# A searched order of 950 steps replaced by another one: the same instructions on all engines, with the groups of many small products kept apart

## The chip, the cores and the metric

The kernel runs on one core of a Trainium2 chip. A core has five engines with a queue of instructions each: PE (TensorE, matmuls and their weight loads), DVE (VectorE), ACT (ScalarE), POOL (GpSimd) and SP (SyncE, which here only issues DMAs). Each engine takes its own queue strictly in order; where an instruction needs what another engine or a DMA makes, it waits for a semaphore, and all that is behind it in its queue waits too. The metric is the device time of one execution in microseconds (us), as a median of several executions. The span of a profile is a little shorter than the time of the execution that it shows.

## The reference

The result is a sum of three terms over a sequence of 2048 tokens with 512 channels: the input itself, a state-space convolution of its layernorm, and a gated linear unit of its layernorm.

```python
x  = A_u                                    # [1, 2048, 512], bf16
xn = _layernorm(x)

# A: diagonal state space, 128 modes a channel, as a convolution of length 2048
dt = exp(log_dt)[:, None]
K  = einsum("dn,dnl,dn->dl", Cc, exp(dt * A * l), dt * Bc).real
y  = irfft(rfft(pad(xn)) * rfft(pad(K)))[:L] + xn * Dskip

# B: gated linear unit, 512 -> 1792 -> 512
g, u = xn @ w_gate, xn @ w_up
b    = (sigmoid(g) * u) @ w_down

return x + y + b
```

## The kernel before

**What is computed how.** The gated unit works on four groups of 512 tokens. For each group there are 14 blocks of 128 hidden units. A block takes four matmuls for the gate (line 1013, 128x512, accumulated over 4 pieces of the 512 channels) and four for the up-projection (L1037). ACT makes the sigmoid of the gate (L1025), DVE multiplies it with the up-projection (L1052). For some blocks ACT first copies the up-projection out of the matmul's memory (L1048), and the product on DVE is then cheaper. The blocks for which that is so are listed in `UEV`. When the 14 products of a group are there, 4 times 14 matmuls (L1086) with `wd_sb`, the weights w_down, make the output.

The convolution is computed by a transform written as small matmuls. The layernormed input goes through a first stage (L683, groups of eight 32-row matmuls), is copied by ACT (L285) and stored to scratch memory in HBM (`z_scr`). From there it is loaded again in 16 units of 256 channels by 8 frequency groups, transformed (L875, four matmuls), multiplied with the transformed kernel (L897 makes the kernel's part from the loaded table `c_E`; DVE multiplies on L902 and L906), transformed back (L919, 16 matmuls) and stored (`v_scr`), to be read at the end by the last stage (L979).

The kernel K of the convolution is made from powers of the 128 modes. This is done four times, for 128 channels each. DVE builds two tables of powers by complex products (L722, L723, L727, L728, with squares from ACT L775). PE then multiplies them in two halves of 64 small products each (L806, 32 columns, 82 moving elements, each with a weight load of its own); ACT or DVE copies both halves out (L285 or L283, 128x656), and PE selects and sorts the entries by 64 more small products (L826). Their result is copied out (128x768), and DVE adds one row to it (L837). L806 and L826 are the groups of many small products. All of these tables, and the transforms' steps, share the two wide buffers `pair0` and `pair1` of the matmul memory.

The layernorm of each 128 tokens ends in a scaling, on DVE (L555) or on ACT (L550), as the list `ON_DVE` says. Tokens from 512 on are transposed by way of HBM: SP stores 512 scaled tokens to `x_scr` (L418), and a transposing load brings them back as `xnT` (L573), which the gate's and up-projection's matmuls of the groups 1 to 3 read.

**What sets the order.** The program builds a list of 950 steps (`pl.add`, `pl.copy`, `dma`), each with its engine and a function that issues its instructions. `ORDER` is a list of the 950 numbers, written out. `_Plan.run` goes through it: it gives each step its buffers from the pools in that order, and the steps' functions are then called one after the other. So `ORDER` fixes the order of instructions in each engine's queue, the order of the DMAs that SP issues, and which buffer of a pool each step has. Nothing reorders it afterwards.

```python
for n in ORDER or range(len(self.ops)):
    op = self.ops[n]
    for s in op.acq:
        s.idx = self.free[s.pool].pop(0)
    for s in op.rel:
        self.free[s.pool].append(s.idx)
    yield op
```

`ON_DVE` lists the steps among the copies and the late layernorm scalings that go to DVE and not to ACT. Of the numbers that it holds, 103 to 132 are scalings, 360 a copy of 128x656, 362 one of 128x768, 516 and 520 ones of 128x1024, and 843 to 853 ones of 128x512.

The DMAs on SP are issued in `ORDER`'s order as well (L418 for all of them, L573 for the transposing loads). `wd_sb` is loaded by one DMA of 1.8 MB.

Of the kernel before, what the change touches and what calls it, by code (L numbers as in the profile page):

```python
# [180 lines left out]
def _consts():  # L181
# [19 lines left out]
UEV = (0, 2, 4, 5, 6, 7, 9, 10, 11, 12, 13, 14, 15, 16, 17, 20, 21, 23, 24, 25, 26, 27, 28, 29, 30, 31, 32, 33, 34, 35, 36, 37, 38, 39, 40, 41, 42, 43, 44, 47, 49, 50, 55,)  # L201
ON_DVE = (103, 105, 116, 132, 360, 362, 516, 843, 853,)
ON_ACT = (2,)
ORDER = [
# [50 lines left out]
class _Plan:  # L255
# [20 lines left out]
    def copy(self, nc, cost, out, in_, *args, **kw):  # L276

        get = lambda v: v() if callable(v) else v
        dve = len(self.ops) in ON_DVE

# [35 lines left out]
def kernel(  # L316
# [214 lines left out]
    def layernorm(i0, i1, prio):  # L531
# [14 lines left out]
        for i in range(i0, i1):  # L546
            dve = i < LN_ACT or len(pl.ops) in ON_DVE
            if not dve:
# [448 lines left out]
    for grp in range(4):  # L997
        hts, prods = [], []
        for u2 in range(7):
# [4 lines left out]
            for k in (2 * u2, 2 * u2 + 1):  # L1004
# [38 lines left out]
                us = _Slot("us")  # L1043
                on = un in UEV

# [136 lines left out]
```

## Time and profile before

| What | Value |
|---|---|
| median of 3 runs | 219.53 us (218.43 to 220.34) |
| the profiled execution's own time | 219.73 us |
| its span | 217.9 us |
| busy PE | 209.3 us (96% of the span), 2098 matmuls |
| busy DVE | 199.7 us (92%), 439 instructions |
| busy ACT | 171.4 us (79%), 277 instructions |
| busy POOL | 33.4 us (15%) |
| bytes moved by DMA | 44.46 MB, 204 GB/s in the mean |

An engine is busy while one of its instructions runs; the rest of the span it waits, or has nothing left. A matmul counts from its start to an end that is modelled, and matmuls overlap, so that the distance from one start to the next says more than the duration of one. In a list of pieces in order of time, a row holds the start, the length, the engine, the line, what it writes and reads, and how many instructions are merged in it; a bracket at its end says how long the engine was idle before it and who ended that. "issue" there means that the profile shows nothing for which the engine waited.

### The profile page before, as it was taken

The numbers are of one execution on the slowest core, as the hardware profiler recorded it, in microseconds if no ns is written. First come the engines' busy times: TensorE is split into PE (matmuls) and PEld (weight loads), VectorE is DVE, ScalarE is ACT, GpSimd is POOL, SyncE is SP. The second block draws the span as 40 slices with busy tenths as digits, with TensorE's granted clock in tenths as the row PEclk, the third lists the DMA queues.
The fourth block names the chain that finished last, engine by engine and source line by source line (L and its number), as shares of the span: only waits on it lengthen the run. The fifth ranks groups of instructions, "written<-read, shape, count | busy, mean of one in ns | idle before, by whom it ended". The sixth has DMA issues, their size and how long they took to land.

```text
span 217.9 us, 5440 instructions
## 1 busy us (share of the span) xinstructions
PE 209.3 (96%) x2098; PEld 104.2 (48%) x2098; DVE 199.7 (92%) x439; ACT 171.4 (79%) x277; POOL 33.4 (15%) x65
## 2 busy tenths in 40 slices
PE   7999999999999999997999999899989999999995
PEld 2654443444444544443655555454546465544453
DVE  4999999999999999999799999999989999984673
ACT  3799999999999997797899999667659979752000
POOL 3125153145104000108100000000010100000200
PEclk9999999999999999999999999999999999999999
DMA  5999999629988678479546343970996876888744
GB/s 173 339 427 433 280 203 161 94 67 191 275 208 182 195 252 237 123 188 288 102 129 205 96 147 87 254 215 3 271 276 144 305 188 200 224 238 222 218 173 144
DMA packets 44044, 44.46 MB, mean 204 GB/s; under 512 B 9449, under 2 KB 35314, under 8 KB 43890
## 3 DMA queue, kind: packets, MB, share of 16 engines
q1 hardware_dynamic: 39330, 39.06, 57.9%
q0 software_dynamic: 4384, 4.73, 13.7%
q10 hardware_dynamic: 304, 0.33, 0.6%
q8 instruction: 16, 0.26, 0.5%
q14 instruction: 10, 0.08, 0.1%
HBM read 25.22 MB, written 12.07 MB: 171 GB/s over the span
## 4 chain that ended last, share of the span: by engine, by line
PE 54%; ACT 23%; DMA 11%; issue 5%; SPq 3%; DVE 2%; POOL 0%; ACTq 0%; POOLq 0%
PE bank L1086 15%; PE bank L1013 10%; PE bank L1037 8%; ACT big L285 8%; PE pair L897 7%; ACT hT_sb L1025 5%; PE pair L919 4%; PE bank L521 3%; ACT us_sb L1048 3%; SPq L418 3%; DMA xnT<-x_scr 2%; DMA x_scr<-big 2%; DMA z_scr<-big 2%; DMA big<-z_scr 2%; ACT big L655 2%
## 5 line engine op out<-in xcount | busy, mean ns | idle before, releaser
L285 ACT ACTIVATE big<-pair 128x1024 bf16<-128x1024 f32 (+2 forms) x73 | 71.1, 1005 | 10.2 <-PE pair L919 3.4
L1037 PE MATMUL bank<-xnT,wu_sb 128*128 128x512 bf16 x224 | 53.9, 380 | 0.0
L1013 PE MATMUL bank<-xnT,wg_sb 128*128 128x512 bf16 (+1 forms) x220 | 51.6, 368 | 0.9 <-DMA xnT<-x_scr 0.5
L1086 PE MATMUL bank<-wd_sb,hT_sb 128*128 128x512 bf16 (+1 forms) x238 | 50.9, 367 | 0.0
L1086 PEld LDWEIGHTS <-hT_sb 128*128 128x128 bf16 x238 | 22.7, 98 | 24.9 <-issue 1.8
L1025 ACT ACTIVATE hT_sb<-bank 128x512 bf16<-128x512 f32 x52 | 31.0, 613 | 4.6 <-PE bank L1013 4.3
L1013 PEld LDWEIGHTS <-wg_sb 128*128 128x128 bf16 x236 | 21.7, 98 | 25.2 <-issue 3.0
L1037 PEld LDWEIGHTS <-wu_sb 128*128 128x128 bf16 x224 | 20.7, 98 | 25.3 <-issue 2.5
L1048 ACT ACTIVATE us_sb<-bank 128x512 bf16<-128x512 f32 x43 | 26.3, 617 | 2.4 <-PE bank L1037 2.4
L722 DVE TENSOR_TENSOR big<-big 128x1024 bf16<-128x1024 bf16 (+4 forms) x40 | 26.5, 663 | 0.7 <-ACT big L285 0.6
L723 DVE TENSOR_TENSOR big<-big 128x1024 bf16<-128x1024 bf16 (+4 forms) x40 | 26.4, 660 | 0.0
L897 PE MATMUL pair<-big 128*128 128x256 bf16 x160 | 19.6, 273 | 0.9 <-DMA big<-c_E 0.9
L902 DVE TENSOR_TENSOR big<-big 128x2048 bf16<-128x2048 bf16 x16 | 19.5, 1220 | 0.4
L897 PEld LDWEIGHTS <-big 128*128 128x128 bf16 x160 | 15.4, 98 | 6.0 <-DMA big<-c_E 1.4
L1052 DVE TENSOR_TENSOR hT_sb<-hT_sb,us_sb 128x512 bf16<-128x512 bf16 x43 | 17.4, 414 | 0.7 <-ACT us_sb L1048 0.7
L660 POOL DMA_DIRECT2D big<-big x24 | 13.1, 551 | 25.4 <-DVE big L666 23.4
L775 ACT ACTIVATE sq_sb<-big 128x256 bf16<-128x256 bf16 (+2 forms) x20 | 13.4, 676 | 3.9 <-DVE big L728 3.9
L727 DVE TENSOR_TENSOR big<-big 128x512 bf16<-128x512 bf16 (+4 forms) x40 | 16.3, 407 | 0.2
L728 DVE TENSOR_TENSOR big<-big 128x512 bf16<-128x512 bf16 (+4 forms) x40 | 16.3, 408 | 0.0
L285 ACT ACTIVATE big<-big 128x256 bf16<-128x256 bf16 x36 | 15.6, 474 | 0.0
L888 DVE COPY big<-big 32x1024 bf16<-32x1024 bf16 x32 | 13.4, 420 | 0.5
L919 PE MATMUL pair<-big 64*64 64x512 bf16 (+1 forms) x256 | 13.0, 326 | 0.2 <-ACT big L285 0.2
(100 smaller groups left out, 214.2 us busy)
## 6 DMA issues: line engine op xcount, KB each, us to landing
big<-c_E SPq DMA_DIRECT2D x16, 320.0 KB, 3.9
z_scr<-big SPq DMA_DIRECT2D x16, 256.0 KB, 3.9
big<-z_scr SPq DMA_DIRECT2D x16, 256.0 KB, 4.2
v_scr<-big SPq DMA_DIRECT2D x16, 256.0 KB, 2.5
big<-big POOLq DMA_DIRECT2D x24, 128.0 KB, 3.6
big<-in_A_u_dram SPq DMA_DIRECT2D x4, 512.0 KB, 6.8
big<-big SPq DMA_DIRECT2D x32, 64.0 KB, 3.3
big<-v_scr SPq DMA_DIRECT2D x4, 512.0 KB, 4.7
```

The source lines that it names most:

```text
L285: nc.scalar.activation(out=get(out), in_=get(in_), func=ACT.Identity)
L722: V.tensor_tensor(out=wide(outp), in0=wide(lo), in1=mre, op=ALU.mult)
L723: V.tensor_tensor(out=wide(tb()), in0=wide(lo), in1=mim, op=ALU.mult)
L897: T.matmul(two(sk)[:, o:o + DW], es()[:, g, kt, :], kT[p][:, kt, :], start=kt in (0, NKT - 1), stop=kt >= NKT - 2)
L902: V.tensor_tensor(out=pp().rearrange("p q h m -> p (q h) m"), in0=xx().rearrange("p q h m -> p (q h) m"), in1=kb()[:, 0:2 * DW].unsqueeze( ...
L919: T.matmul(two(sv)[o:o + 64, DW * (2 * g + y):2 * DW * (g + 1)], mab[b:b + 64, 2 * u + g, q, :], pq()[b:b + 64, q, ch] if y else pp()[b:b ...
L1013: T.matmul(bank(sl, k % 2)[:, c0:c1], w_at(w, CUT_G, kt, k), xnT[:, grp, kt, c0:c1], start=(kt == 0), stop=(kt == KT - 1))
L1025: S.activation(out=hT_sb[:, hs.idx, k % 2, :], in_=bank(sl), func=ACT.Sigmoid)
L1037: T.matmul(bank(sl), w_at(wu_sb, CUT_U, kt, k), xnT[:, grp, kt, :], start=(kt == 0), stop=(kt == KT - 1))
L1048: S.activation(out=us_sb[:, us.idx, :], in_=bank(sl), func=ACT.Identity)
L1052: V.tensor_tensor(out=h(), in0=h(), in1=us_sb[:, us.idx, :] if on else bank(sl), op=ALU.mult)
L1086: T.matmul(bank(po)[:, 0:c[1] - c[0]], hT_sb[:, hts[k // 2].idx, k % 2, jj * 128:(jj + 1) * 128], wd_sb[:, k, c[0]:c[1]], start=first and ...
```

## The change

`ORDER` is another order of the same 950 steps. `UEV` and `ON_DVE` change with it. Everything else in the file is the same. Both kernels issue the same transfers and the same matmuls.

```diff
-UEV = (0, 2, 4, 5, 6, 7, 9, 10, 11, 12, 13, 14, 15, 16, 17, 20, 21, 23, 24, 25, 26, 27, 28, 29, 30, 31, 32, 33, 34, 35, 36, 37, 38, 39, 40, 41, 42, 43, 44, 47, 49, 50, 55,)
-ON_DVE = (103, 105, 116, 132, 360, 362, 516, 843, 853,)
+UEV = (0, 1, 2, 3, 4, 5, 6, 7, 9, 10, 11, 14, 15, 16, 17, 18, 19, 20, 21, 22, 23, 26, 27, 28, 29, 30, 31, 32, 33, 34, 35, 36, 37, 38, 39, 40, 41, 42, 44, 45, 50, 51, 52, 54, 55,)
+ON_DVE = (104, 105, 106, 119, 129, 362, 520, 843, 851,)
 ORDER = [
-    1, 0, 19, 2, 4, 3, 31, 6, 10, 32, 23, 34, 7, 33, 39, 24, 5, 25, 35, 26, 36, 11, 40, 37, 13, 20, 27, 41, 9, 51, 28, 12,
...
-    902, 931, 597, 847, 855, 930, 848, 934, 929, 856, 849, 857, 591, 932, 935, 933, 683, 675, 936, 938, 684, 937, 676,
...
+    0, 1, 20, 2, 3, 4, 23, 6, 19, 10, 24, 31, 26, 7, 25, 39, 32, 5, 33, 27, 34, 40, 11, 28, 13, 51, 35, 41, 9, 29, 36, 30,
...
+    592, 597, 847, 855, 848, 934, 856, 849, 929, 930, 857, 591, 683, 675, 684, 935, 932, 938, 676, 685, 933, 677, 936, 937,
...
```

What moves with it, as far as the prediction speaks of it:

- Between the two halves of L806 and the L826 that follows, PE has other groups in its queue. Their matmuls, for the four times: 56, 12, 32 and 24 in the old order, 56, 20, 38 and 36 in the new one. In the second time these are four of L1013, four of L1037 and four of L875 in the old order, and five groups of four of L1013 or L1037 in the new one. In the fourth they are 16 of L919, four of L875 and four of L1013 in the old order; the new one adds two large groups and one of L875.
- On SP, `wd_sb` (step 16) stands before the first store to `x_scr` (step 107) in the old order, and behind that store and the first transposing load (step 108) in the new one. The last 512 tokens of the input (step 15) are loaded before that store and not behind it.
- On DVE, the products of the first token group stand in another order among the products and scalings that build the power tables. Ahead of the fourth L806, DVE has the same steps in both orders, except for one scaling more and one product that goes from the dearer to the cheaper kind.
- `UEV` has 45 blocks where it had 43. `ON_DVE` has five late scalings (it had four), one copy of 128x768, one of 128x1024 and two of 128x512 (as before), and no longer the one of 128x656.

75 rows, old and new, of the table ORDER are left out of this document.

## The prediction

> **What bounds the kernel now.** I read the page first, then the busy time by stretches, then the idle pieces of TensorE (PE), the stretches around its groups of small products, and the waits of VectorE (DVE).
>
> ```profile
> span 217.9 us, 5440 instructions
> PE 209.3 (96%) x2098; PEld 104.2 (48%) x2098; DVE 199.7 (92%) x439; ACT 171.4 (79%) x277; POOL 33.4 (15%) x65
> ...
> 60.00:80.00 20.00, 20.00 (x239) 8.96 (x238) 20.00 (x53) 20.00 (x36) 2.63 (x8) 1.00 0.81 214
> ...
> 100.00:120.00 20.00, 18.46 (x185) 10.19 (x183) 18.59 (x39) 17.71 (x33) 4.05 (x7) 1.00 0.61 166
> 120.00:140.00 20.00, 19.39 (x325) 10.11 (x323) 19.93 (x52) 18.76 (x33) 0.35 (x2) 1.00 0.47 131
> 140.00:160.00 20.00, 18.53 (x320) 10.11 (x321) 18.98 (x36) 12.86 (x18) 0.00 (x0) 1.00 0.67 194
> ```
>
> The columns of a stretch are its length, then busy PE, weight loads, DVE, ACT, POOL, clock, DMA. Two engines are full at once: PE 209.3 of 217.9 us, and DVE 20.00 of 20 us at 60 to 80, 19.93 at 120 to 140. The granted clock is 1.00 throughout. So the time is PE's 209.3 plus what PE stands idle, and DVE is close behind. PE's idle pieces, in brackets with the releaser:
>
> ```profile
> 1.43 4.84 PE L521 MATMUL bank<-glu_sb 128*128 128x512 bf16 x14 [1.43 <-POOL glu_sb L514]
> 16.91 1.89 PE L1013 MATMUL bank<-xnT,wg_sb 128*128 128x512 bf16 x8 [0.17 <-ACT hT_sb L1025]
> 35.28 1.04 PE L1013 MATMUL bank<-xnT,wg_sb 128*128 128x512 bf16 x4 [0.49 <-DMA xnT<-x_scr]
> 102.89 0.47 PE L826 MATMUL pair<-big,sw 128*32 128x96 bf16 x26 [1.53 <-issue]
> 140.25 1.26 PE L897 MATMUL pair<-big 128*128 128x256 bf16 x10 [0.86 <-DMA big<-c_E]
> 155.19 0.84 PE L919 MATMUL pair<-big 64*64 64x512 bf16 x16 [0.21 <-ACT big L285]
> 159.10 0.31 PE L826 MATMUL pair<-big,sw 128*32 128x96 bf16 x12 [1.02 <-issue]
> ```
>
> They add up to 5.7 us; the rest of 217.9 - 209.3 = 8.6 is, but for tenths, the end, after PE's last matmul. The two largest behind the start fall inside a selection group (L826, 64 matmuls), with no releaser. Beside them stand the kernel-table products (L806, 128 matmuls with a weight load each) that precede each selection:
>
> ```profile
> 73.94 1.50 PE L806 MATMUL pair<-big 128*32 128x82 bf16 x128
> ...
> 85.03 0.86 PE L826 MATMUL pair<-big,sw 128*32 128x96 bf16 x64
> ...
> 97.23 1.42 PE L806 MATMUL pair<-big 128*32 128x82 bf16 x128
> 98.58 1.04 PE L1013 MATMUL bank<-xnT,wg_sb 128*128 128x512 bf16 x4
> 99.45 1.03 PE L1037 MATMUL bank<-xnT,wu_sb 128*128 128x512 bf16 x4
> 100.41 0.41 PE L875 MATMUL pair<-big,m 64*64 64x512 bf16 x4
> 100.75 0.60 PE L826 MATMUL pair<-big,sw 128*32 128x96 bf16 x38
> ...
> 126.17 1.59 PE L806 MATMUL pair<-big 128*32 128x82 bf16 x128
> ...
> 131.48 0.86 PE L826 MATMUL pair<-big,sw 128*32 128x96 bf16 x64
> ...
> 153.57 1.41 PE L806 MATMUL pair<-big 128*32 128x82 bf16 x128
> ...
> 157.35 0.74 PE L826 MATMUL pair<-big,sw 128*32 128x96 bf16 x52
> ```
>
> From the start of L806 to the start of its L826 there are 11.09, 3.52, 5.31 and 3.78 us. The second and fourth stalled, after 38 and 52 of 64 matmuls; the others ran through in 0.86. So it is the crowding that stalls, and the point lies between 3.78 and 5.31 us.
>
> What runs out is, I argue, instructions.
>
> ```profile
> q8 instruction: 16, 0.26, 0.5%
> ```
>
> 16 packets carry 0.26 MB; PE has 2 x 2098 instructions, so one packet is about 262 of them, which L806 alone (256) uses up in 1.4 us.
>
> The Trainium skill (Runtime: NRT & Kernel Launch, section Instruction fetch mechanics) gives the block as 16 KiB or 256 instructions, which this row bears out. The same section says that fetching is hidden, because dispatch is slower than the fill, and gives PE a store of 2048 instructions; by that the 1.53 and 1.02 would have another cause and the order would leave them, the third rival below. The rows speak against it: both stalls come only in the crowded groups.
>
> **The change, part by part.**
>
> *Spacing.* In the new order five groups of four 128x512 matmuls stand between the second L806/L826 pair where L1013, L1037 and L875 stood. A large group takes 99.45 - 98.58 = 0.87, L875 0.34 (100.41 to 100.75), so the distance becomes 3.52 - 0.34 + 3 x 0.87 = 5.8. The fourth gains two large groups and one L875: 3.78 + 2 x 0.87 + 0.34 = 5.9. The third goes from 32 matmuls between to 38, the first stays. All are beyond the 5.31 that ran through. Removed: 1.53 + 1.02 = **2.55** of PE. If a stall were only shortened, the loss is bounded by these.
>
> *What is late next: DVE.* The fourth L806 waits for DVE, as its first weight load shows; and DVE was itself idle in front of the two rows below it, and of the last one after it:
>
> ```profile
> 153.57 1.27 PEld L806 LDWEIGHTS <-big 128*32 128x32 bf16 x128 [0.42 <-DVE hT_sb L1052]
> ...
> 104.25 0.28 DVE L837 TENSOR_TENSOR big<-pair,dskr 1x128 bf16<-1x128 f32 x1 [0.78 <-ACT big L285]
> ...
> 107.03 0.39 DVE L722 TENSOR_TENSOR big<-big 128x256 bf16<-128x256 bf16 x1 [0.56 <-ACT big L285]
> ...
> 159.53 0.96 DVE L283 CAST big<-pair 128x768 bf16<-128x768 f32 x1 [0.69 <-PE pair L826]
> ```
>
> L837 comes after ACT's copy of what the stalled L826 makes, so 0.78 of DVE's idle time is the stall passed on; the 0.56 that follows within 3 us, also behind ACT, may be. DVE's work ahead of 153.57 changes too. The page's groups give the prices:
>
> ```profile
> L1052 DVE TENSOR_TENSOR hT_sb<-hT_sb,us_sb 128x512 bf16<-128x512 bf16 x43 | 17.4, 414 | 0.7 <-ACT us_sb L1048 0.7
> L1048 ACT ACTIVATE us_sb<-bank 128x512 bf16<-128x512 f32 x43 | 26.3, 617 | 2.4 <-PE bank L1037 2.4
> L1052 DVE TENSOR_TENSOR hT_sb<-hT_sb,bank 128x512 bf16<-128x512 bf16 x13 | 8.6, 679 | 1.0 <-PE bank L1037 1.0
> L550 ACT ACTIVATE big<-big,ln_nb_f,ln_ri_f 128x512 bf16<-128x512 bf16 x8 | 6.5, 831 | 0.0
> L555 DVE TENSOR_SCALAR big<-big,ln_m_f,ln_ri_f 128x512 bf16<-128x512 bf16 x8 | 3.1, 404 | 0.1
> L285 ACT ACTIVATE big<-pair 128x656 bf16<-128x656 f32 x7 | 5.1, 750 | 1.9 <-PE pair L806 1.9
> L283 DVE CAST big<-pair 128x656 bf16<-128x656 f32 x1 | 0.8, 842 | 0.2 <-ACT big L285 0.2
> ```
>
> Five late layernorm scalings instead of four go to DVE: +0.40 there, -0.83 on ACT. Two more products read a copy made by ACT: 2 x (0.414 - 0.679) = -0.53 on DVE, 2 x 0.617 = +1.23 on ACT. One 128x656 copy goes over to ACT: -0.84 and +0.75. The other copies change places one for one. Sum: DVE -0.97, ACT +1.15; ACT has 46 us free. Ahead of the fourth L806 stand 37 cheap products and 5 dear ones instead of 36 and 6, and the extra scaling: 0.40 - 0.27 = +0.14. So DVE is there 0.78 - 0.14 = 0.64 earlier, or 1.20 with the 0.56. PE has the same matmuls ahead of it in both orders, and keeps only that much of its 1.53; I take **1.0**, nearer the upper end, since the 0.56 stands right behind the stall. PE's idle pieces before 153.57 (0.17, 0.49, 1.53, 0.86) are 3.05: with 1.0 of it gone, some 2 us of waits in that stretch are still free, whether the 0.86 for c_E or new ones.
>
> After 153.57 the second stall's **1.02** is kept whole if DVE follows. It loses its 0.69 at 159.53 and the 0.84 copy, and is 1.5 earlier there on top of its lead, so it does.
>
> *SP's queue.* The 1.8 MB load of wd_sb, issued among the first loads now, is moved behind the first x_scr store and the first transposing load, which waits for that store. In the profile (chain, then DMA issues, then the tile wd_sb):
>
> ```profile
> 24.32 5.43 DMA x_scr<-big
> 29.81 5.43 DMA xnT<-x_scr
> ...
> wd_sb<-in_B_w_down_dram SPq DMA_DIRECT2D x1, 1792.0 KB, 16.2
> ...
> L1086 PE MATMUL bank<-wd_sb,hT_sb x238: 272/379/391, 37.9 to 214.3; 128*128 128x512 bf16 x105, 128*128 128x256 bf16 x14
> ```
>
> The store needs the same scalings as before, so it goes at about 24, the transposing load at about 28 to 30, wd_sb right behind. PE's first L1086 has one large group and one of eight L683 more ahead of it: 37.9 - 0.49 + 0.87 = 38.3 and some tenths, about 38.6. Landing is bounded by nothing gained below (a load that is there before 38.6 gains nothing now either) and by 30 + 16.2 = 46.2 above, a wait of 7.6. In the 16.2 it stood behind the other weights and inputs on the same queue; in the new order those are issued long before it. The nearest row is the 512 KB transposing load's 5.43: the same bytes a us give 19, which holds for 2-byte pieces and not for rows of 14 KB. I take it as hidden, just in time, and keep 7.6 as a bound.
>
> The Trainium skill (DMA: Bandwidth & Descriptors, section Queues, rings and completion order) says that each DMA engine consumes one queue's descriptors in ring order; by that wd_sb starts only when the transposing load is through, near 33 to 35. No row of this profile shows the order inside a queue. By it the load would have 4 to 6 us left before PE asks, which is the second rival's case.
>
> *Small waits.* The two late products that feed the first L1086 (its 2nd and 11th matmul) stand about 8 and 9 us later in DVE's order, by the durations of the rows ahead of them, and come within half a us of PE's need. That is up to 0.5 of PE, inside the 2 us that are free. The other loads keep 3 us or more between issue and use, or what they have now.
>
> **The sum.** The profiled execution took 219.73 with its span of 217.9, so 1.83 lie around the span. 219.73 - 1.0 - 1.02 = 217.7, and the median of the runs shown (219.53) is 0.20 lower: **217.5 us**.
>
> **The rivals.**
>
> 1. *Given back in tenths.* DVE, ACT and PE hand over within a few tenths everywhere (gaps of 0.56 to 0.78 above are the largest), and a whole new order makes new gaps. For: both engines are full, so each gap costs. Against: the old order, as full, shows only those. One 0.5 gap in each of the four kernel-table stages costs 2.0: 219.53.
> 2. *Slower: wd_sb late.* One place, PE's first L1086. It decides from a landing later than 38.6 plus the 2 us that are free, 10.6 us after an issue at 30. At 16.2 the wait is 7.6; less the 2.55 of stalls, less about 0.5, which the other early waits then no longer cost, it gives 219.5 + 4.5 = 224.
> 3. *It doesn't do what it says.* The stall isn't a matter of spacing, or moves on to another group: 2.55 stays, 219.5, less a few tenths for the lighter DVE.
>
> **How the numbers follow.** Forecast 0.55, from 216.4 to 218.6: 0.64 to 1.53 kept of the first stall, all or half of the second, and half a us of spread between executions (the runs shown lie from 218.43 to 220.34). Rival 1 has 0.20 (218.6 to 220), rival 2 0.15 (220 to 224), rival 3 0.10 (219 to 220). The range is 216.4 to 221.0; it leaves out most of rival 2 and little else. One per cent, about what a measurement of this kernel can tell from no change, is 2.2 us: faster means below 217.3, three fifths of the forecast's cases (0.9 of 2.2 us of its span, and the denser part of it), 0.33. Slower means above 221.7, most of rival 2 and a little for a cause that I don't see, 0.14. Within one per cent is the rest, 0.53.
>
> **What would show it.** No idle piece with the releaser "issue" before L826, and four L826 groups of 64 in about 0.86. Busy time per engine: PE 209, DVE about 199, ACT about 172.5. The fourth L806 starts 0.6 to 1.2 earlier than 153.57, the last stage about 2 earlier. The first L1086 starts within 1 us of 38.6; a wait for wd_sb there, a longer DVE idle sum between 30 and 150, or an "issue" row with another small group would each make the forecast wrong.

## The result, and the profile after

The new order takes **217.49 us** (median of 15 executions, 216.14 to 219.46). The old one takes 219.50 beside it (15, 218.33 to 220.34). The ratio is **0.9914, with a 95% interval of 0.9892 to 0.9935**; 217.5 was predicted. The profiled execution took 217.89 us with a span of 216.1, where the old order's took 219.73 with 217.9. One remark that some numbers below need: in e1, e2, e5, e6, e10 and e11, and in the old order beside them, some executions had a granted clock of 0.992 in place of 1.0 and mostly took 1 to 3 us longer, so the medians in the table below are of the executions at the full clock (only e1's counts two of its four at 0.992, and the ratios of e1, e5 and e6 contain some).

The page of the new order, the span and the busy times:

```profile
span 216.1 us, 5430 instructions
...
PE 210.2 (97%) x2098; PEld 104.6 (48%) x2098; DVE 198.2 (92%) x439; ACT 172.3 (80%) x279; POOL 31.5 (15%) x65
```

PE is busy 0.9 us longer than before and DVE 1.5 less; PE's share has risen from 96% to 97%. The repeat of the new order (e9) has 208.8 for PE, so the 0.9 is within what executions of one order differ by. Next, in PE's list in order of time, stand the second and the fourth pair of L806 and L826, and every idle piece of over 0.2 from the first L1086 on (start, length, then the group, and in brackets the idle time before it):

```profile
41.81 10.10 PE L1086 MATMUL bank<-wd_sb,hT_sb 128*128 128x512 bf16 x46 [0.29 <-DVE hT_sb L1052]
...
96.61 1.48 PE L806 MATMUL pair<-big 128*32 128x82 bf16 x128
...
102.44 0.86 PE L826 MATMUL pair<-big,sw 128*32 128x96 bf16 x64
...
108.79 1.02 PE L1013 MATMUL bank<-xnT,wg_sb 128*128 128x512 bf16 x4 [0.38 <-ACT hT_sb L1025]
...
127.47 0.80 PE L806 MATMUL pair<-big 128*32 128x82 bf16 x64 [0.27 <-ACT big L285]
...
130.67 0.41 PE L875 MATMUL pair<-big,m 64*64 64x512 bf16 x4 [0.22 <-DMA big<-z_scr]
...
152.59 1.65 PE L806 MATMUL pair<-big 128*32 128x82 bf16 x128
...
158.46 0.86 PE L826 MATMUL pair<-big,sw 128*32 128x96 bf16 x64
```

Both "issue" pieces are gone, and both groups of L826 run through with 64 matmuls in 0.86. The distances from L806 are 102.44 - 96.61 = 5.83 and 158.46 - 152.59 = 5.87 us. The other large piece of the old order is gone too: no group waits for c_E any more. The largest that is left behind the start is 0.38 in this execution; the repeat of the same order (e9) has one of 1.36.

The early part, where wd_sb moved: DVE's list, the chain of waits between 20 and 45 us, the tile wd_sb and the DMA issues of the new order:

```profile
39.33 0.69 DVE L664 SCALAR_TENSOR_TENSOR big<-big 128x512 f32<-128x512 f32 x1 [0.64 <-DMA big<-big]
```

```profile
29.42 9.82 DMA big<-big
```

```profile
L1086 PE MATMUL bank<-wd_sb,hT_sb x238: 272/379/390, 39.2 to 212.5; 128*128 128x512 bf16 x105, 128*128 128x256 bf16 x14
L418 SPq DMA_DIRECT2D wd_sb<-in_B_w_down_dram x1: 555/555/555, 29.2 to 29.2; - x1
```

```profile
wd_sb<-in_B_w_down_dram SPq DMA_DIRECT2D x1, 1792.0 KB, 9.8
```

The load is issued at 29.2 and is there 9.8 us later, at about 39.0. PE's first L1086 starts at 39.2. POOL's copy of the power ladder, issued beside it, takes 9.82 us, and DVE waits 0.64 for it.

### The profile page after: what moved, and what is told of

Read it like the earlier page. It is cut to its first block, busy times and chain, and to the rows that moved or that the text cites. A ratio compares the mean times of both kernels' runs of the same rounds, so it can differ in the third digit from the quotient of the medians.

```text
span 216.1 us, 5430 instructions
## 1 busy us (share of the span) xinstructions
PE 210.2 (97%) x2098; PEld 104.6 (48%) x2098; DVE 198.2 (92%) x439; ACT 172.3 (80%) x279; POOL 31.5 (15%) x65
## 4 chain that ended last, share of the span: by engine, by line
PE 46%; DVE 25%; ACT 12%; DMA 11%; issue 3%; SPq 0%; POOL 0%; ACTq 0%; DVEq 0%
PE bank L1086 16%; PE bank L1037 10%; PE bank L1013 6%; ACT big L285 5%; PE pair L897 5%; DMA big<-big 5%; PE pair L919 4%; DVE big L722 4%; DVE big L723 3%; ACT hT_sb L1025 3%; DMA v_scr<-big 3%; DVE big L603 3%; DVE stats L542 3%; DMA big<-z_scr 2%; DVE big L727 2%
## 5 line engine op out<-in xcount | busy, mean ns | idle before, releaser
L1037 PE MATMUL bank<-xnT,wu_sb 128*128 128x512 bf16 x224 | 54.0, 380 | 0.0
L1013 PE MATMUL bank<-xnT,wg_sb 128*128 128x512 bf16 (+1 forms) x220 | 50.9, 368 | 0.4 <-ACT hT_sb L1025 0.4
L1086 PE MATMUL bank<-wd_sb,hT_sb 128*128 128x512 bf16 (+1 forms) x238 | 50.6, 367 | 0.4 <-DVE hT_sb L1052 0.3
L1086 PEld LDWEIGHTS <-hT_sb 128*128 128x128 bf16 x238 | 22.4, 98 | 25.9 <-issue 2.1
L1013 PEld LDWEIGHTS <-wg_sb 128*128 128x128 bf16 x236 | 22.0, 98 | 25.2 <-issue 3.7
L1037 PEld LDWEIGHTS <-wu_sb 128*128 128x128 bf16 x224 | 20.8, 98 | 24.8 <-issue 2.6
L1025 ACT ACTIVATE hT_sb<-bank 128x512 bf16<-128x512 f32 x52 | 30.1, 610 | 1.2 <-PE bank L1013 1.1
L1048 ACT ACTIVATE us_sb<-bank 128x512 bf16<-128x512 f32 x45 | 27.4, 622 | 2.7 <-PE bank L1037 2.7
L897 PE MATMUL pair<-big 128*128 128x256 bf16 x160 | 19.6, 273 | 0.0
L1052 DVE TENSOR_TENSOR hT_sb<-hT_sb,us_sb 128x512 bf16<-128x512 bf16 x45 | 18.5, 419 | 1.1 <-ACT us_sb L1048 1.0
L897 PEld LDWEIGHTS <-big 128*128 128x128 bf16 x160 | 15.5, 98 | 4.6 <-issue 0.7
L727 DVE TENSOR_TENSOR big<-big 128x512 bf16<-128x512 bf16 (+4 forms) x40 | 16.6, 415 | 0.1
L728 DVE TENSOR_TENSOR big<-big 128x512 bf16<-128x512 bf16 (+4 forms) x40 | 16.6, 415 | 0.0
L542 DVE BATCH_NORM_STATS2 stats<-big 128x6 f32<-128x512 bf16 x15 | 10.2, 680 | 3.7 <-DMA big<-in_A_u_dram 3.7
```

The lines of the kernel that those rows point to most:

```text
L727: V.tensor_tensor(out=outp[:, :, 0], in0=outp[:, :, 0], in1=tb()[:, :, 1], op=opr)
L897: T.matmul(two(sk)[:, o:o + DW], es()[:, g, kt, :], kT[p][:, kt, :], start=kt in (0, NKT - 1), stop=kt >= NKT - 2)
L1013: T.matmul(bank(sl, k % 2)[:, c0:c1], w_at(w, CUT_G, kt, k), xnT[:, grp, kt, c0:c1], start=(kt == 0), stop=(kt == KT - 1))
L1025: S.activation(out=hT_sb[:, hs.idx, k % 2, :], in_=bank(sl), func=ACT.Sigmoid)
L1037: T.matmul(bank(sl), w_at(wu_sb, CUT_U, kt, k), xnT[:, grp, kt, :], start=(kt == 0), stop=(kt == KT - 1))
L1048: S.activation(out=us_sb[:, us.idx, :], in_=bank(sl), func=ACT.Identity)
```

## The experiments

The times of all of them, in us. Each is compared with the old order on its own chip, so the ratio is what can be compared between rows.

| Kernel | median | old order beside it | ratio, 95% interval |
|---|---|---|---|
| new order | 217.49 | 219.50 | 0.9914 [0.9892, 0.9935] |
| new order again (e9) | 217.71 | 220.27 | 0.9882 [0.9831, 0.9932] |
| e1: new order, PE's queue shifted by 102 instructions | 223.41 | 219.68 | 1.0166 [1.0127, 1.0206] |
| e2: old order, the same shift | 220.09 | 219.68 | 0.9998 [0.9966, 1.0029] |
| e3: old order, only the spacing | 220.07 | 219.68 | 1.0009 [0.9985, 1.0033] |
| e4: new order, crowded again | 220.26 | 219.68 | 1.0012 [0.9974, 1.0049] |
| e5: new order, wd_sb early | 218.33 | 219.84 | 0.9965 [0.9931, 0.9999] |
| e6: new order, DVE 2.4 more | 220.17 | 219.84 | 1.0039 [1.0005, 1.0073] |
| e7: new order, DVE 2.4 less | 216.88 | 219.84 | 0.9872 [0.9831, 0.9913] |
| e8: new order, PE 2.6 more | 219.15 | 219.84 | 0.9974 [0.9948, 0.9999] |
| e10: old order, DVE 2.4 less | 219.14 | 220.27 | 0.9954 [0.9924, 0.9984] |
| e11: the same with the spacing | 219.67 | 220.27 | 0.9972 [0.9948, 0.9997] |
| e12: old order, spacing and its consumers | 219.50 | 220.27 | 0.9972 [0.9946, 0.9997] |

### Is it the distance, or the place in the instruction stream? (e1, e2)

In PE's queue of the old order the two stalled matmuls lie 766 matmuls apart. With their weight loads these are 1532 instructions, and a few others of PE stand between them: that is six blocks of 256. The distance theory doesn't ask for that; a fetch in blocks does. So 17 of the warm-up matmuls, whose result nobody uses, are each cut in four. Nothing else changes but the count of instructions ahead of everything that follows, and the length of the warm-up: the first L806 starts at 76.03 in e1 (75.30 in the new order) and at 74.70 in e2 (73.94 in the old one).

```diff
-            for _ in range(n):
-                T.matmul(bank(wsl), glu_sb[:, 0, 0:128], glu_sb[:, 0, :], start=True, stop=True)
+            for w in [128] * (4 * min(n, {14: 14, 6: 3}.get(n, 0))) + [D] * (n - {14: 14, 6: 3}.get(n, 0)):
+                T.matmul(bank(wsl)[:, 0:w], glu_sb[:, 0, 0:128], glu_sb[:, 0, 0:w], start=True, stop=True)
```

> The new order, with 17 of the 20 first warm-up matmuls (L521, 128x512, their result is never used) each split into four of 128x128: 51 matmuls and their 51 weight loads more, 102 instructions on PE, at about the same time, long before anything waits for PE. Every later PE instruction has the same neighbours and the same distances, but its number in the queue is 102 higher. Theory A (PE's instructions arrive in blocks of about 256, by q8's 16 packets; PE stalls where it runs through a whole block in less than some 5.2 us; so it counts where the borders between blocks fall): borders now fall so that a whole block is used within 1.6 to 3.3 us around the second, third and fourth L806. Idle pieces with the releaser issue appear behind these, near 97, 127 and 154 us, of about 3.5, 3.4 and 1.8 us, none of them in L826 of the second group; the time rises by 4 to 8.7 us, to 221.5 to 226. Theory B (only the distance from a group of L806 to its L826 counts, as the prediction put it): no issue piece, 217.5, within 0.5.

PE's list of the new order with the shift. Some records of matmuls are missing in this trace, so that a count can be a few short, with an idle piece of 0.16 in its place; such pieces are left out here:

```profile
97.33 1.45 PE L806 MATMUL pair<-big 128*32 128x82 bf16 x128
...
100.84 1.46 PE L1013 MATMUL bank<-xnT,wg_sb 128*128 128x512 bf16 x6 [1.52 <-issue]
...
104.82 0.86 PE L826 MATMUL pair<-big,sw 128*32 128x96 bf16 x64
...
127.92 1.42 PE L806 MATMUL pair<-big 128*32 128x82 bf16 x127
132.12 0.20 PE L806 MATMUL pair<-big 128*32 128x82 bf16 x1 [2.77 <-issue]
...
160.78 0.82 PE L1037 MATMUL bank<-xnT,wu_sb 128*128 128x512 bf16 x3 [0.70 <-issue]
```

Three stalls are back in an order that had none, all with the distances of the new order. None is in L826. They lie inside a large group of 128x512 matmuls, ahead of the last of 128 matmuls of L806, and inside another large group. Theory B is out. The sum of 1.52 + 2.77 + 0.70 = 4.99 is smaller than the 8.7 that theory A gave, so the places were right and the sizes were not. The time is 223.41, some 5.6 us above what the new order would take on this chip (an estimate, 0.9914 x 219.68 = 217.79). Of that, 0.73 is the longer warm-up. From the first L806 to PE's last L1086 it is 138.69 us here, 134.27 in the new order and 134.78 in its repeat e9: 3.9 to 4.4 of the 4.99 are paid, so here a stall costs most of its length.

> The old order with the same 102 PE instructions more in the warm-up. Theory A: the two stalls of 1.53 and 1.02 inside L826 leave their places; instead about 3.3 us right behind the second L806 (near 97.6), about 2.3 behind the third (near 127 to 130, where the old order had none), about 1.8 at the start of the fourth L826; sum about 7.4 where it was 2.55, the time 2.5 to 5 us above 219.5. Theory B: the same 1.53 and 1.02, after 38 and 52 of 64 matmuls of L826, and 219.5 within 0.5.

The old order with the shift, the same list:

```profile
97.80 1.50 PE L806 MATMUL pair<-big 128*32 128x82 bf16 x128
...
101.40 0.86 PE L826 MATMUL pair<-big,sw 128*32 128x96 bf16 x64
...
128.22 0.73 PE L919 MATMUL pair<-big 64*64 64x512 bf16 x11
130.67 0.38 PE L919 MATMUL pair<-big 64*64 64x256 bf16 x5 [1.72 <-issue]
...
157.93 0.22 PE L826 MATMUL pair<-big,sw 128*32 128x96 bf16 x1
159.71 0.86 PE L826 MATMUL pair<-big,sw 128*32 128x96 bf16 x63 [1.56 <-issue]
```

The fourth L826 stalled after 52 matmuls before; with 51 more ahead it stalls after 1. The third group, which ran through, now stalls inside L919. The second pair, 101.40 - 97.80 = 3.60 us apart, runs through, and theory A expected 3.3 us of stall there: a miss. By the starts of the weight loads, the 128 ahead of that border were used in 1.3 us (an estimate), and those ahead of the two stalls of e2 in an estimated 2.5 and 3.6. So how long a block takes to come varies, by more than the theory has room for. The time did not move (theory A had it 2.5 to 5 longer) although the stalls went from 2.55 to 3.28. In the old order, a wait of 0.86 for c_E followed at 140.25; in e2 no matmul waits for c_E, so part of the 1.72 may stand in the place of that wait.

The traces record every weight load of PE, so the stalls' places can be counted. These are the weight loads ahead of each stall (e4 and e10 to e12 are described further down):

| Kernel | weight loads ahead of each stall |
|---|---|
| old order, e10 | 861, 1627 |
| e1 | 861, 1244, 1627 |
| e2 | 1244, 1627 |
| e4, e11, e12 | 1627 |

They are always the same three places, 383 weight loads apart, or 766 instructions with the matmuls: three blocks of 256, less a few other instructions. Which group of the program stands there differs. The queue "q8 instruction" fits: 17 packets and 0.28 MB in e1 and e2, 16 packets in all other kernels. Counted back 128 weight loads from each place (one block, an estimate), PE used the block in 1.2 to 3.6 us where it stalled, or in 4.8 where it stalled for 0.34 and 0.41 (e11, e12); with the stall it is 4.3 to 5.4 us, once 3.5. In the new order these three blocks are used in 5.6, 8.0 and 5.3 us. Three were used in under 4.9 us without a stall: 1.3 in e2, 4.0 in e4 and 4.8 in e3.

The Trainium skill (Runtime: NRT & Kernel Launch, section Instruction fetch mechanics) has the blocks of 256 and says that the fetch is hidden, because dispatch is slower than the fill. The first agrees with the places of the stalls here; the second doesn't: in e1, 4.99 us of stalls came with 102 instructions more.

### The spacing alone, and taken away (e3, e4)

e3 moves L826 (steps 267 and 361) back in PE's queue of the old order, by 1.74 and 1.21 us of other groups; all other engines keep their order.

```diff
-    ... 385, 175, 824, 386, 366, 472, 825, 267, 441, 288, 823, 473, 461, 289, 789, 826, 460, 292, 268, 837, 474,
+    ... 385, 175, 824, 386, 366, 472, 825, 441, 288, 823, 473, 461, 289, 789, 826, 460, 292, 837, 267, 268, 474,
...
-    ... 560, 425, 361, 546, 889, 523, 534, 898, 362, 410,
+    ... 560, 425, 546, 889, 523, 534, 898, 361, 362, 410,
```

> The old order; only on PE, and only in two places, L826 is moved back in the queue: the second behind one L1037 and one L1013 group more (1.74 us of matmuls), the fourth behind one L875 and one L1013 group more (1.21). Every other engine keeps its order, and L826 ends about when it ended with its stall. Both theories A and B: the two issue pieces go (at most 0.3 left at the fourth, where the distance is 5.0 only). What it tells apart is where the gain comes from. If PE alone bounds the stretch (C), the time falls by all of 2.55, to 217.0. If DVE holds PE on a leash (D, the prediction's), DVE still gets the second L826's copy no earlier, keeps its 0.78 of idle time in front of L837, and the fourth L806 starts within 0.3 of 153.57; of the second stall at most 1.0 is kept: 218.5 to 219.5. If the rest of the new order makes the gain and the stalls do not matter (E): 219.5.

The two idle pieces with the releaser "issue" are gone. PE's list of e3:

```profile
102.72 0.86 PE L826 MATMUL pair<-big,sw 128*32 128x96 bf16 x64
...
104.90 2.34 PE L897 MATMUL pair<-big 128*128 128x256 bf16 x20 [0.34 <-DVE big L837]
...
139.94 1.26 PE L897 MATMUL pair<-big 128*128 128x256 bf16 x10 [1.08 <-DMA big<-c_E]
...
153.27 1.42 PE L806 MATMUL pair<-big 128*32 128x82 bf16 x128
...
160.78 1.25 PE L897 MATMUL pair<-big 128*128 128x256 bf16 x10 [0.48 <-DVE big L837]
```

The 2.55 us are removed and the time stays, 1.0009 [0.9985, 1.0033]. Part of the stalls comes back as waits: 0.34 and 0.48 for DVE's L837, and the wait for c_E has grown from 0.86 to 1.08. That last wait is the one that PE's later work hangs on. In the chain of waits of the *old* order, between 95 and 165 us, the path is on PE until 113.9, with the stall on it, and then leaves it:

```profile
101.35 1.53 issue
...
113.92 0.60 ACT hT_sb L1025
...
123.45 1.97 DMA big<-big
...
126.75 1.13 DVE big L902
...
132.95 1.38 SPq L418
...
136.85 3.35 DMA big<-c_E
...
140.25 1.26 PE pair L897 x10
```

It runs over ACT, a DMA, DVE, ACT again, and SP, which issues its transfers one after the other (SPq), to the load of c_E. PE is not on it for 26 us, so what PE gains in that stretch is lost at 140. The stall at 101.35 lies ahead of it, and its removal should have moved the whole chain. The chain of e3 shows why it did not:

```profile
102.79 0.91 PE pair L826 x64
103.72 0.82 ACT big L285
104.56 0.29 DVE big L837
104.90 1.26 PE pair L897 x10
...
109.02 2.29 DMA big<-big
...
113.35 0.60 ACT hT_sb L1025
```

The moved L826 ends at 102.72 + 0.86 = 103.58; with its stall it had ended at 103.36. So ACT's copy and DVE's L837, which need its result, come no earlier (104.56 for 104.25), and the path now runs over them, over the L897 that waits for L837, and over a transfer behind it. ACT's L1025 is 0.57 earlier, the load of c_E 0.34 (issued at 136.51 for 136.85). So this spacing turned the idle piece into work and left the delay of the consumers. The fourth L806 follows the L897 at 140.25 with PE full: 153.57 - 140.25 = 13.32 us in the old order, 153.27 - 139.94 = 13.33 in e3. The expectation of at most 0.3 was right there; of the second stall's 1.02 nothing reached the time either.

e4 does the opposite in the new order: L826 ahead of the last two or three groups that stand between, and ACT's copy 264 moved ahead so that it is there in time.

```diff
-    ... 384, 266, 807, ... 277, 794, 833, 387, 264, 812, 441, ... 283, 267, 290,
+    ... 384, 266, 264, 807, ... 277, 794, 833, 387, 267, 812, 441, ... 283, 290,
...
-    ... 888, 436, 865, 560, 425, 437, 534, 854, 878, 866, 501, 571, 879, 361, 572,
+    ... 888, 436, 361, 865, 560, 425, 437, 534, 854, 878, 866, 501, 571, 879, 572,
```

> The new order; on PE the second L826 is moved ahead of two L1013 groups and the fourth ahead of one L1037, one L1013 and one L875 group; ACT's copy of the other half of the second L806 is moved ahead of three other ACT steps, so that it is there in time. Distances from L806 to L826 about 4.1 and 3.8 in place of 5.83 and 5.87. Theories A and B: the issue pieces return inside L826, about 1.0 and 1.3 us, in the 2nd and 4th group. Time: with PE as the bound 219.5 to 220; by the leash (D) 218 to 219, since L826 still ends no later than in the new order and its consumers on ACT and DVE are not later. If the stalls have nothing to do with the distance (third rival of the prediction): no issue piece, 217.5.

PE's list of e4:

```profile
95.69 1.44 PE L806 MATMUL pair<-big 128*32 128x82 bf16 x128
...
99.75 0.86 PE L826 MATMUL pair<-big,sw 128*32 128x96 bf16 x64
...
155.11 0.74 PE L826 MATMUL pair<-big,sw 128*32 128x96 bf16 x52
157.32 0.31 PE L826 MATMUL pair<-big,sw 128*32 128x96 bf16 x12 [1.48 <-issue]
```

The fourth group stalls again, after 52 matmuls as in the old order. The second, 99.75 - 95.69 = 4.06 us behind its L806, runs through in this execution, against both theories. The ratio is 1.0012, over seven executions with a median of 220.26 (220.62 over all ten), so the gain is lost, and more than was expected (218 to 220); but this profiled execution took only 218.47, and the executions lie between 218.47 and 222.19, a wide spread. What the longer ones contain was not seen. That a second stall, which comes in some of them, is the reason would fit and is not shown.

### Who bounds the new order (e6, e7, e8)

The first two change DVE's work ahead of the fourth L806, on four multiplications of the power tables. In e7 they are left out, so the tables of the last 128 channels are not the reference's.

```diff
-            V.tensor_tensor(out=wide(tb()), in0=wide(lo), in1=mim, op=ALU.mult)
+            for _ in range(2 if n == 4 and prio in (PCH[3], PCH[3] - 0.5) else 1): V.tensor_tensor(out=wide(tb()), in0=wide(lo), in1=mim, op=ALU.mult)
```

```diff
-            V.tensor_tensor(out=wide(tb()), in0=wide(lo), in1=mim, op=ALU.mult)
+            if n != 4 or prio not in (PCH[3], PCH[3] - 0.5): V.tensor_tensor(out=wide(tb()), in0=wide(lo), in1=mim, op=ALU.mult)
```

e8 does three groups of L1037 twice.

```diff
-                    for kt in range(KT):
+                    for kt in (*range(KT), *range(KT)) if grp == 2 and k in (13, 6, 8) else range(KT):
```

> The new order with DVE work added ahead of the fourth L806: in the tables for the last 128 channels each of the four multiplications L723 on 128x1024 is done twice (same result), 4 x 0.60 = 2.4 us of DVE. PE's order and work are the same. Leash (D): the fourth L806 and all behind it come later by most of it; 1.5 to 2.4 us, 219 to 220. PE alone is the bound (C): DVE has some slack, at most 0.5 later, 217.5 to 218.

> The new order with DVE work left out ahead of the fourth L806: the same four multiplications L723 on 128x1024 are not done, so the kernel tables of the last 128 channels are not the reference's; 2.4 us of DVE less. Leash (D): PE's waits there shrink, but PE is close behind: its idle pieces between 105 and 154 in the new order are 0.38, 0.27 and 0.22, so at most 0.9 earlier, 216.6 to 217.2. PE alone (C): 217.5 within 0.2.

> The new order with PE work added between 105 and 154: three groups of four L1037 are done twice (same result), 3 x 0.87 = 2.6 us of PE, 24 instructions. If PE is the bound there now (C): 2.4 to 2.6 later, 220. If DVE is the bound and PE only follows (D): PE takes up part of it in its waits, 0.5 to 1.7 later, 218 to 219.2. By theory A the borders of the blocks behind it move by 24 only and no stall appears.

The fourth L806 in e6, e7 and e8, one row of PE's list from each:

```profile
155.00 1.67 PE L806 MATMUL pair<-big 128*32 128x82 bf16 x128 [2.26 <-DVE big L727]
```

```profile
151.29 1.42 PE L806 MATMUL pair<-big 128*32 128x82 bf16 x128
```

```profile
153.85 1.42 PE L806 MATMUL pair<-big 128*32 128x82 bf16 x128
```

The new order has it at 152.59 (152.79 in e9). 2.4 us more on DVE put it 2.41 later, with a wait of 2.26 that names DVE; 2.4 us less bring 1.3. On the chip of these three the new order would take about 0.9914 x 219.84 = 217.95 (an estimate; 217.5 to 218.4 by the interval of the ratio); e6 is 2.2 above it, e7 1.1 below, e8 with 2.6 us more on PE 1.2 above. So in the new order DVE stands right behind PE, as the leash (D) has it, and PE takes up half of its extra work in its waits. The bound on PE's idle pieces for e7 (0.9) was slightly too tight.

### Whether wd_sb should go back (e5)

```diff
-    ... 47, 599, 8, 50, 605, ... 115, 69, 658, 16, 667, 616,
+    ... 47, 599, 8, 16, 50, 605, ... 115, 69, 658, 667, 616,
```

> The new order with one step moved: the load of wd_sb is issued on SP ahead of the first x_scr store again, as in the old order. In the new order it was issued at 29.24 and landed 9.8 us later, at 39.05, just ahead of PE's first L1086 at 39.20; beside it POOL's copy of the power ladder issued at 29.42 took 9.82 us in place of some 3.6, and DVE waited 0.64 for it at 39.33, PE 0.29 for a late product at 41.81. Theory F (the load slows POOL's copy, and that is where 0.3 to 0.6 of the gain was lost): the copy takes 3 to 5 us again, the 0.64 goes, the time falls by 0.2 to 0.6, to 216.9 to 217.3. Theory G (early waits are free, since PE has waits behind them anyway): the 0.64 goes and the time stays, 217.5 within 0.2. If the load's early place costs more elsewhere (a first group of weights later): above 217.7.

A row of PE's list and the DMA issue of wd_sb in e5:

```profile
35.13 1.04 PE L1013 MATMUL bank<-xnT,wg_sb 128*128 128x512 bf16 x3 [1.34 <-DMA xnT<-x_scr]
```

```profile
wd_sb<-in_B_w_down_dram SPq DMA_DIRECT2D x1, 1792.0 KB, 15.8
```

The 0.64 on DVE goes, and the load needs 15.8 us again. In its place the transposing load comes late, and PE waits 1.34 for it. The time is 218.33, 0.4 above the estimated 217.95 and inside its 217.5 to 218.4. Theory F is out: the time doesn't fall. Whether the early waits are free (G) this run can't tell, since one of 1.34 took the place of the other; that the early place costs a little elsewhere would fit as well. The place of wd_sb in the new order is no worse than the old one, as far as this run resolves it.

### Is the old order held by DVE? (e9 to e12)

e9 is the new order once more; e10 is the old one with the four multiplications of e7 left out (the same channels' tables are not the reference's); e11 adds e3's spacing to that; e12 is e3, all work done, with DVE's L837 and the next L897 moved back too.

```diff
-    ... 460, 292, 837, 267, 268, 474, 290, 269, 790, 278, 787, 287, 389, 788, ... 476, 784, 465,
+    ... 460, 292, 837, 267, 268, 474, 290, 790, 278, 269, 787, 287, 784, 389, 788, ... 476, 465,
...
-    ... 898, 361, 362, 410, 903, 899, 363, 437, 503, 853, 904, 524, 561, 878, 504,
+    ... 898, 361, 410, 903, 899, 437, 362, 363, 878, 503, 853, 904, 524, 561, 504,
```

(This diff is against e3.)

> The new order itself, unchanged, on the same chip as the three that follow. All theories: 0.9914 of the kernel before, within 0.4%; no issue piece of over 0.2 us in PE's list. It is the measure for the others.

> The old order, with the four multiplications L723 on 128x1024 in the tables of the last 128 channels left out (so the kernel tables of those channels are not the reference's): 2.4 us of DVE less ahead of the fourth L806; both stalls stay. In the old order PE has 0.86 of waits for c_E and the 0.42 that its weight loads wait for DVE ahead of the fourth L806; the stall itself, 1.53, is not given up. Theory H (in the old order DVE holds PE, so the stall was hidden behind DVE's lateness; with DVE lighter PE's stalls become the bound): 0.5 to 1.3 below the kernel before. Theory I (the stalls cost nothing whatever DVE does): 1.0 to 2.0 below, and the same as the next kernel.

> The same, with L826 moved back on PE in the two places as in the spacing experiment, so that the stalls are gone; the same four multiplications are left out. Spacing alone gave nothing (ratio 1.0009). Theory H: with DVE lighter the two stalls are worth PE time, so this is 1.0 to 2.5 below the kernel with the lighter DVE and the stalls, 2 to 3 below the kernel before. Theory I: within 0.4 of the kernel with the lighter DVE and the stalls.

> The old order, all work done; the spacing of the two L826 as before, and beside it only what lets DVE and the next group on PE use it: DVE's step that adds the row (L837) is moved behind one table step of 1.2 us in the second place, and the copy and that step behind one L906 in the fourth; on PE the next L897 is moved behind one large group more in both places. In the spacing experiment DVE idled 0.47 and 0.92 there, and PE 0.34 and 0.48 for L837. Theory D (DVE's idle pieces in front of the selection's consumers are what kept the removed stalls from paying): these four pieces shrink to under 0.3 each, the time falls by 0.5 to 1.4 below the kernel before. Theory E (only the rest of the new order, spread over all stages, makes the gain): the same as the spacing experiment, within 0.3 of the kernel before.

e9 repeats the gain, 0.9882 [0.9831, 0.9932], with no "issue" piece. One row of its PE list differs from the first execution's, a late load that cost PE 1.36; the fourth L806 starts at 152.79 all the same, 0.2 later:

```profile
95.01 0.63 PE L875 MATMUL pair<-big,m 64*64 64x512 bf16 x8 [1.36 <-DMA big<-z_scr]
```

The wait for c_E and the fourth L806 behind it, PE's lists of e10 and e12:

```profile
139.43 1.26 PE L897 MATMUL pair<-big 128*128 128x256 bf16 x10 [0.72 <-DMA big<-c_E]
...
152.76 1.42 PE L806 MATMUL pair<-big 128*32 128x82 bf16 x128
```

```profile
139.98 1.26 PE L897 MATMUL pair<-big 128*128 128x256 bf16 x10 [0.93 <-DMA big<-c_E]
...
153.31 1.41 PE L806 MATMUL pair<-big 128*32 128x82 bf16 x128
```

In e11 the two start at 139.76 and 153.09. In all six versions of the old order the fourth L806 starts 13.3 us behind that L897: PE runs without a pause between them. In five of them that L897 waited for c_E; in e2 it did not (154.15 - 140.82). So where the wait stands, the landing of c_E sets the fourth L806.

Theory H is out: with DVE lighter, the spacing is worth nothing (219.67 against 219.14, even a little dearer; 0.34 of the fourth stall is left in e11). Theory I has that right, but its 1.0 to 2.0 for the lighter DVE is at the lower end, 1.1. That the lighter DVE made this 1.1 is not shown: in e10's trace three of the four multiplications that are left out would come behind the wait for c_E (145.62, 149.03 and 150.86 in the old order). The fourth L806 is 0.81 earlier there, but 0.68 of that has been gained when the chain reaches ACT's L1025 at 113.24, ahead of all four: this time the stall was 1.13 in place of 1.53, and the first L806 had started 0.17 earlier. There an earlier c_E went with a shorter stall.

Moving the consumers too (e12) gives 0.8 of the 0.5 to 1.4 that D expected, though not as D had it: the waits for L837 are gone, a wait of 0.75 for ACT's us_sb stands in their place at 105, DVE still waits 0.69 for the fourth L826, in which 0.41 of the stall is left, and the wait for c_E stays. Its trace is as long as e3's (219.60 both), and the intervals of the two ratios overlap, so that it is faster than e3 is not certain.

## Why the prediction was right, and where it was not

**The stalls go: right.** Distances of 5.83 and 5.87 stand against 5.8 and 5.9, there is no "issue" piece, and all four groups run through.

**Their cause: half right.** That instructions run out holds (e1, e2, and the same three places in every trace with a stall). That "it is the crowding that stalls, and the point lies between 3.78 and 5.31 us" from L806 to L826 does not: 3.60 (e2) and 4.06 (e4) ran through, and with the new order's distances three stalls came from 102 instructions more far ahead. There is no such point of distance; what counts is how fast PE runs from one border of 256 instructions to the next, and where the borders lie. That the new order has no fast block at those places is luck as far as the prediction goes, which didn't count them.

**The first term, 1.0: right in size, wrong in reason.** The fourth L806 starts at 152.59 in place of 153.57, 0.98 earlier (0.78 in e9). The prediction had DVE as the one that holds PE back there in the old order, by the wait of its first weight load, and counted the 0.86 for c_E among waits that "are still free". That is the step that failed. The wait for c_E was the end of a chain that begins with PE's stall, runs over ACT, DVE and SP, and held PE: the fourth L806 starts 13.3 us behind the landing, with PE full between. With the stalls removed, L826's end left where it was and that wait left (e3), 0.3 of the 1.53 reached the fourth L806 and none the end. In the new order nothing waits for c_E (nor for any other load between 105 and 154, but for 0.22 for z_scr), and PE pays for most of a stall there (e1). So, as far as these runs show, the gain takes both, the spacing and an order in which what follows L826 isn't late. The prediction priced the first as if the second were there. That it was is luck: no step of the sum looks for it.

**The second term, 1.02: about right.** The last stage starts 1.8 earlier, so 0.8 came behind the fourth L806. DVE follows, as predicted; its wait of 0.69 is gone.

**DVE and ACT: right within about half a us.** DVE's busy time fell by 1.5 (predicted 0.97), ACT's rose by 0.9 (1.15). That "DVE is close behind" is borne out by e6.

**wd_sb: right, and just in time indeed.** Issue at 29.2 (28 to 30 was said), landing 9.8 us later (between nothing and 16.2), first L1086 at 39.2 (38.6, within 1). Not foreseen was that the load slows POOL's ladder copy to 9.82, which costs DVE 0.64. PE paid 0.29 of that or of the late product (up to 0.5 was said), and in e5 the old place is no cheaper.

**The rivals.** "Given back in tenths" did not come; the largest new wait on PE is 0.38, or 1.36 in e9, whose time is the same. wd_sb was not late. "The stall isn't a matter of spacing" is true of the mechanism, as e1 shows, and the stalls went nevertheless: in the new order no block happens to be used too fast (5.3 us or more at the three places).

**What stays open.** Which part of the rest of the new order lets the spacing pay was not taken apart; that the c_E wait alone, taken out of the old order, would do it was not tried. Nor is it shown why the time for a block varies: borders that should have stalled for 3.3 us (e2) and about 1 us (e4) did not. What makes up the 0.8 of e12 and the 1.1 of e10 is open.

## What to carry to other kernels

Before a removed stall is counted as gained, follow the chain of waits past it: moving the stalled group later fills the idle piece and leaves its consumers where they were (e3), and a wait for a DMA further on may look like free slack and be the end of that same chain. If an engine stops in a burst of small instructions with no releaser, add harmless instructions far ahead of it (102 here) and count; if the stall stays at the same count while the program moves under it, it is the instruction stream, and a reorder that works may work only until the next edit shifts the count. Where two engines are full, test each with a little work more and a little less: here 2.4 us on DVE cost 2.2 and saved 1.1.

## What the runs showed of the hardware

- PE stopped at the same counts of its instructions, 861, 1244 or 1627 weight loads from the start, whatever group stood there (1.52 and 0.70 us inside groups of large matmuls in e1), where it had used the 128 weight loads and matmuls ahead in 1.2 to 3.6 us, and a little (0.34, 0.41) after two of three blocks of 4.8; two blocks of 1.3 and 4.0 us did not stall it. 102 instructions more in the warm-up, some 90 us and more earlier, cost about 5.6 us at the end (an estimate), 0.7 of them in the warm-up.
- The 1.8 MB load of wd_sb took 16.2 and 15.8 us when it was issued early among the others, and 9.8 when it was issued at 29. POOL's copy issued 0.2 us behind it then took 9.82 us, and in the repeat e9 9.78, where the median of these copies is 3.4; in e5, with the load early, the same copy took 3.0.
